# Softmax chain of a channel-attention kernel split by row block, with the square root on GpSimd, the row sums applied after the product with W, and the transposes of v as tasks of their own

## The chip, the cores and the metric

The kernel runs on one core of a Trainium2 chip. The time is the device time of one execution in microseconds (us). Of the core's engines these do the work here: TensorE (PE: matrix products and transposes, which it writes to PSUM), VectorE (DVE) and ScalarE (ACT) for elementwise work, GpSimd (POOL), which issues the loads, and SyncE (SP), which issues the stores. Each engine runs its own instructions strictly in the order in which the program lists them; a wait on one instruction holds all those behind it.

## The reference

Four batches of q, k and v, each 6336 x 256 in float32. Attention is over the 256 channels, not over the rows; a highway layer with two 256 x 256 matrices follows.

```python
qn = q / (np.linalg.norm(q, axis=1, keepdims=True) + 1e-06)
kn = k / (np.linalg.norm(k, axis=1, keepdims=True) + 1e-06)
s = kn.transpose(0, 2, 1) @ qn / tau
s = s - s.max(-1, keepdims=True)
a = np.exp(s)
a /= a.sum(-1, keepdims=True) + 1e-09
x = (v @ a).reshape(-1, 256)            # 25344 rows
H = np.maximum(x @ w_h, 0.0)
T = 1.0 / (1.0 + np.exp(-(x @ w_t + b_t)))
return T * H + (1.0 - T) * x
```

## The kernel before

**Stage 1** (`stage1`, lines 365 to 380) walks over the 6336 rows of a batch in 50 blocks of 128 (the last two of 96) and accumulates in two PSUM banks, `sg0` and `sg1`, one for each half of the 256 channels of k: the product of k and q (line 376, 256 columns), and the squares of k and of q (lines 377 and 378, 128 columns each), whose diagonals are the squared norms. q, k and v come in by loads of 8 row blocks (1 MB of float32 in memory, cast to float16 on the way), all issued by POOL in a fixed order, 8 of them in flight at most.

**The chain** (`plan_chain`, lines 386 to 639) then turns the sums of one batch into the operands `mr` of stage 2, once per batch. In order: four diagonals (DVE, line 413); the copy of the k-q product out of PSUM, which frees `sg0` and `sg1` for the next batch (ACT, line 433); the square root, for the first batch by one ACT instruction and a load of the table for the exponential (lines 440 and 441), for the other three by a shift, a first guess and three Newton steps on DVE, 13 small instructions in a row (lines 450 to 503); the reciprocal (518); two diagonal matrices (523), which a product with ones (`cqb`, PE, 535) spreads over the partitions; the scaling of the product (540, DVE) and the exponential of both halves (548, ACT), which also gives the row sums; their reciprocals (561, 571) and the normalised a (580 or 578), the first third of `mr`; four transposes of it (593), a copy out of PSUM (603 or 605), the product with both W (`ah`, 612), and its copy into the other two thirds of `mr` (623 or 625). Three of PSUM's users share the one bank `vt`: `cqb`, the four transposes, and the transposes of v of stage 2.

**Stage 2** (`plan_stage2`, lines 834 to 906) takes 25 groups of two row blocks per batch, 100 in all. Per group: transposes of v (line 657, two float16 channels at a time as one float32 word) into `vt`, their copy to `vtsb` (663 ACT or 665 DVE), and on PE three products of four matmuls each (line 686): h = x w_h, t = x w_t + b, and d, which completes x on top of relu(h)/2. ACT does relu (733) and tanh (747), DVE the two last steps (754 and 773); t begins as a copy of the bias (663 or 665) or, for some of the late groups, by a matmul (724). The transposes for the group two further on stand between the matmuls of h (`main_h`, line 692; `between` in `products`, line 680), so a task `h` also needs the bank `vt` free, and a buffer of `vtsb`.

**The order** of the instructions of each engine is found before the program is written, by `Plan.run` (lines 71 to 175): a simulation with a duration for every task, in which a free engine takes the ready task with the lowest key. Stage 2 has its group number g as key, stage 1 of the next batch keys spread over the groups of the batch before (`slot_of`), the chain -50, so it goes first wherever it is ready. A task that is ready only late on the chip still stands at its planned place. The tasks of POOL and SP, loads and stores, are kept in their listed order (`in_order`, line 85).

## Time and profile before

| | |
|---|---|
| median of 3 runs (lowest to highest) | 294.47 us (294.36 to 294.88) |
| the profiled execution: its time / the span of its instructions | 294.81 us / 293.0 us |
| busy: PE, ACT, DVE, POOL | 264.5, 192.4, 172.0, 48.8 us |
| mean TensorE clock granted, as a share of full speed | 0.974 |
| loads and stores | 39.20 MB (as float16) and 25.95 MB |

The page of the profile has one execution. "Busy" counts the time in which an engine has an instruction in work; matmuls overlap in the pipeline, so their durations (270 ns for 256 columns) are longer than the distance from one start to the next. In a timeline a row gives start, duration, engine, line, operation, output and inputs, and in brackets the idle time ahead of it and what ended it. A view by windows gives busy time per engine in a stretch of the span, the granted clock and the share of the DMA engines in use.

### The profile page before, as it was taken

To read this page: it belongs to the slowest core of one execution; us is meant where nothing else is said; L and a number is where in the kernel's file an instruction comes from. 1 tells how busy PE (TensorE), PEld (TensorE's weight loads), DVE (VectorE), ACT (ScalarE), POOL (GpSimd) and SP (SyncE) were. 2 spreads that over 40 slices of the span, in tenths; PEclk is the share of its full clock that TensorE was granted. 3 is DMA by queue.
4 is the path that set the end of the run, shared out by engine and by line. 5 is a ranking of instruction groups with operands and counts; after the bars stand their busy time and mean duration, and the time that the engine had idled before them with its cause. 6 is when DMAs were issued, how large, how long until landed. Compare 5 with 4: busy or idle time off the path is not lost.

```text
span 293.0 us, 6605 instructions
## 1 busy us (share of the span) xinstructions
PE 264.5 (90%) x2660; PEld 234.3 (80%) x2660; DVE 172.0 (59%) x343; ACT 192.4 (66%) x396; POOL 48.8 (17%) x96
## 2 busy tenths in 40 slices
PE   0787869999999989999999899999985899999993
PEld 0676847999999879999898789999973688888882
DVE  1000042455555874555658756655668599999995
ACT  1000042778877576888886667888784788889882
POOL 7212542221121221211211221111000010000000
PEclk9997988999999999999999999999997799999999
DMA  6999999999999999999999999999997264335444
GB/s 120 213 214 209 213 209 213 214 213 284 282 246 251 282 215 283 239 269 274 247 256 283 245 251 266 240 286 274 233 285 205 84 144 178 139 145 214 164 182 189
DMA packets 16687, 65.58 MB, mean 224 GB/s; under 512 B 1936, under 2 KB 3600, under 8 KB 13712
## 3 DMA queue, kind: packets, MB, share of 16 engines
q0 software_dynamic: 12608, 39.20, 67.9%
q1 hardware_dynamic: 4048, 25.95, 22.0%
q8 instruction: 21, 0.34, 0.5%
q14 instruction: 10, 0.08, 0.1%
HBM read 78.38 MB, written 25.95 MB: 356 GB/s over the span
## 4 chain that ended last, share of the span: by engine, by line
PE 75%; DMA 13%; DVE 8%; issue 1%; POOL 1%; ACT 1%; DVEq 0%; ACTq 0%; POOLq 0%
PE h L686 15%; PE t L686 14%; PE d L686 14%; PE sg L376 10%; PE vtps L657 8%; PE sg L377 5%; PE sg L378 5%; DMA k<-in_k_dram 5%; DMA q<-in_q_dram 5%; DMA btb<-in_moe_b_t_dram 3%; DVE pp L754 2%; DVE o L773 2%; PE t L724 1%; PE ah L612 1%; DVE gs L540 1%
## 5 line engine op out<-in xcount | busy, mean ns | idle before, releaser
L686 PEld LDWEIGHTS <-vtsb 128*128 128x128 f16 (+1 forms) x1200 | 114.8, 100 | 13.6 <-issue 2.2
L376 PE MATMUL sg<-q,k 128*128 128x256 f16 x384 | 96.1, 281 | 12.8 <-DMA k<-in_k_dram 12.8
L754 DVE SCALAR_TENSOR_TENSOR pp<-uu,d 128x512 f32<-128x512 f32 (+1 forms) x100 | 68.5, 685 | 52.2 <-PE d L686 50.2
L377 PE MATMUL sg<-k 128*128 128x128 f16 x384 | 86.4, 225 | 0.0
L378 PE MATMUL sg<-q 128*128 128x128 f16 x384 | 85.3, 222 | 0.0
L686 PE MATMUL h<-mr,vtsb 128*128 128x256 f16 (+1 forms) x400 | 82.8, 275 | 0.2
L747 ACT ACTIVATE uu<-t 128x512 f32<-128x512 f32 (+1 forms) x100 | 59.7, 597 | 27.3 <-PE t L686 26.8
L773 DVE SCALAR_TENSOR_TENSOR o<-h,pp 128x512 f32<-128x512 f32 x96 | 66.2, 691 | 3.1
L686 PE MATMUL d<-mr,vtsb 128*128 128x256 f16 (+1 forms) x400 | 60.5, 274 | 1.0 <-ACT d L733 1.0
L686 PE MATMUL t<-mr,vtsb 128*128 128x256 f16 (+1 forms) x400 | 60.8, 275 | 0.2
L733 ACT ACTIVATE d<-h 128x512 f32<-128x512 f32 (+1 forms) x100 | 59.5, 595 | 1.4 <-PE h L686 1.2
L657 PE MATMUL vtps<-ident,v 128*128 128x128 f32 x192 | 48.0, 278 | 3.6 <-DVE gs L540 3.4
L376 PEld LDWEIGHTS <-k 128*128 128x128 f16 x384 | 38.3, 100 | 15.2 <-DMA k<-in_k_dram 13.3
L378 PEld LDWEIGHTS <-q 128*128 128x128 f16 x384 | 38.6, 101 | 5.5
L377 PEld LDWEIGHTS <-k 128*128 128x128 f16 x384 | 38.6, 101 | 2.1 <-issue 0.3
L663 ACT COPY vtsb<-vtps 128x256 f32<-128x256 f32 (+1 forms) x91 | 33.4, 368 | 8.6 <-PE vtps L657 6.7
L663 ACT COPY t<-bias_all 128x512 f32<-128x512 f32 (+1 forms) x64 | 37.8, 590 | 2.0
L657 PEld LDWEIGHTS vtps<-ident,v 128*128 128x128 f32 x192 | 27.2, 142 | 8.9 <-DVE gs L540 4.3
L413 DVE SCALAR_TENSOR_TENSOR junk<-sg,ident 128x128 f32<-128x128 f32 x16 | 4.6, 290 | 35.6 <-PE sg L378 34.9
L274 POOL DMA_DIRECT2D v<-in_v_dram x24 | 12.8, 532 | 76.5 <-PE h L686 45.0
L440 ACT ACTIVATE inv<-x 128x4 f32<-128x4 f32 x1 | 0.2, 206 | 38.0 <-DVE junk L413 38.0
L274 POOL DMA_DIRECT2D k<-in_k_dram x25 | 13.3, 533 | 44.1 <-DMA k<-in_k_dram 16.0
(66 smaller groups left out, 121.5 us busy)
## 6 DMA issues: line engine op xcount, KB each, us to landing
out_dram<-o SPq DMA_DIRECT2D x23, 1024.0 KB, 8.9
v<-in_v_dram POOLq DMA_DIRECT2D x24, 512.0 KB, 20.7
q<-in_q_dram POOLq DMA_DIRECT2D x23, 512.0 KB, 21.7
k<-in_k_dram POOLq DMA_DIRECT2D x23, 512.0 KB, 20.6
out_dram<-o SPq DMA_DIRECT2D x2, 512.0 KB, 3.5
out_dram<-ot SPq DMA_DIRECT2D x4, 192.0 KB, 6.4
q<-in_q_dram POOLq DMA_DIRECT2D x2, 256.0 KB, 14.4
k<-in_k_dram POOLq DMA_DIRECT2D x2, 256.0 KB, 11.5
```

Of the source, the lines that this page charges most:

```text
L274: nc.gpsimd.dma_start(out=t[:, s : s + n, :], in_=main_rows(src)[:, j * CH + s : j * CH + s + n, :])
L376: nc.tensor.matmul(sg[c][:, 0:C], kc, qa, start=first, stop=False)
L377: nc.tensor.matmul(sg[c][:, C : C + P], kc, kc, start=False, stop=False)
L378: nc.tensor.matmul(sg[c][:, C + P : C + 2 * P], qa[:, cs], qa[:, cs], start=False, stop=last)
L413: nc.vector.scalar_tensor_tensor(out=st["junk"], in0=sg_t[b][c][:, off : off + P], scalar=0.0, in1=ident0, op0=AluOp.bypass, op1=AluOp.mul ...
L657: nc.tensor.transpose(ps[:, u, 0:nr], words, ident0[0:nr, 0:nr])
L663: nc.scalar.copy(out=out, in_=in_)
L686: nc.tensor.matmul(out[0:nr, u, :], vt[u][kt][:, 0:nr], mr[kt][:, col * C : (col + 1) * C], **flags(u, kt))
L733: nc.scalar.activation(out=d[0:nr, :, :], in_=ps_t["h", b, i][0:nr, :, :], func=Act.Relu, scale=0.5)
L747: nc.scalar.activation(out=uu[0:nr, :, :], in_=ps_t.pop(("t", b, i))[0:nr, :, :], func=Act.Tanh, scale=-0.5)
L754: nc.vector.scalar_tensor_tensor(out=pp[0:nr, :, :], in0=el.pop(("uu", b, i))[0:nr, :, :], scalar=1.0, in1=ps_t.pop(("d", b, i))[0:nr, :, ...
L773: nc.vector.scalar_tensor_tensor(out=ot, in0=ps_t.pop(("h", b, i))[0:nr, :, :], scalar=0.0, in1=el.pop(("pp", b, i))[0:nr, :, :], op0=AluO ...
```

## The change

Seven edits. (1) For every batch the square root is `x ** 0.5` on POOL, in two instructions of 128 x 2: one for the norms of q (`norm(0)`), one for those of k (`norm(2)`); the Newton steps, the square root on ACT and the table loaded for it go. (2) The diagonals are two tasks, q then k; the copies `gs` wait for the second. The reciprocals are two as well: that for q stands with the diagonal matrices ahead of `cqb`, that for k is only needed by the exponential. (3) Scaling, exponential, row sums and what follows are tasks by halves c = 0 and 1. (4) The exponentials themselves, in float32 and not yet divided by the row sums, are transposed (4 float32 transposes), copied to `et` and multiplied by W; the division is done by the copy of `ah` into `mr` (multiplied by `ri`), and the first third of `mr` takes the factor -0.5. (5) The copies of `et` and `ah` go to ACT or DVE, whichever the plan finds free. (6) The transposes of v are PE tasks of their own with key g - 1.6 (`LOOK`), `main_h` is its four matmuls alone, and no longer needs `vt`; the copy of `vt` has key g - 1.5, where it had g - 2.1. (7) In the plan POOL takes a ready task of the chain ahead of a load, and from the start of the fourth block before the last of a stage 1 until the second square root is done it issues no load (`holds`).

```diff
-LOOK = 2
+LOOK = 1.6
+POW = 1.0
...
         def pick(e):
-            if e in in_order:
-                lst = in_order[e]
-                return lst[-1] if lst and ready(lst[-1]) else None
-            return min(
+            best = min(
                 (x for x in avail[e] if ready(x)), key=lambda x: (x.key, x.n), default=None
             )
+            lst = in_order.get(e)
+            if best is None and lst and ready(lst[-1]) and not (e == "POOL" and held()):
+                return lst[-1]
+            return best
+
+        def held():
+            return any(
+                a.start is not None and (b.done is None or b.done > t + eps) for a, b in self.holds
             )
...
+        def norm(n):
+            nc.gpsimd.tensor_tensor(
+                out=st["inv"][:, n : n + 2], in0=st["x"][:, n : n + 2], in1=half, op=AluOp.pow
+            )
+
+        def recip(n):
+            inv = st["inv"][:, n : n + 2]
+            nc.vector.tensor_scalar(
+                out=inv, in0=inv, scalar1=1e-6, scalar2=None, op0=AluOp.add, op1=AluOp.bypass
+            )
+            nc.vector.reciprocal(out=inv, in_=inv)
...
-        x = dve(diagonals, 1.34, 1.4, [last, consts])
+        dq = dve(lambda: (diagonal(0), diagonal(1)), 0.75, 0.8, [last, consts])
+        nq = pool(lambda: norm(0), POW, POW + 0.2, [dq])
+        dk = dve(lambda: (diagonal(2), diagonal(3)), 0.75, 0.8, [dq])
+        nk = pool(lambda: norm(2), POW, POW + 0.2, [dk])
+        plan.holds.append((plan.tasks[plan.tasks.index(last) - 3], nk))
...
-        gs = act(copy_g, 0.58, 0.7, [diag], drop=[(first, "sg0"), (first, "sg1")])
...
-            last_steps = [floor, shift, guess] + [n1, n2, n3] * 3 + [root]
...
-        inv = x = several(last_steps + [eps, recip, lambda: dcat(0), lambda: dcat(1)], x)
+        gs = act(copy_g, 0.58, 0.7, [dk], drop=[(first, "sg0"), (first, "sg1")])
+        iq = dve(lambda: (recip(0), dcat()), 0.82, 0.92, [nq, dk])
+        ik = dve(lambda: recip(2), 0.3, 0.36, [nk])
...
-        cqb = x = pe(bcast, 0.85, [x], take=["vt"])
+        cqb = pe(bcast, 0.43, [iq], take=["vt"])
+        cqb.lat = 0.85
...
+        def soft(c):
...
+            nc.vector.tensor_scalar(
+                out=mr_t[b][c][:, 0:C],
+                in0=st["e"][:, c, :],
+                scalar1=st["ri"][:, c : c + 1],
+                scalar2=-0.5,
+                op0=AluOp.mult,
+                op1=AluOp.mult,
+            )
+
+        def trans(c):
+            if c == 0:
+                st["eps"] = new("vt", [P, 2, 2, P], f32, f"eps{b}")
+                st["et"] = small.tile([P, 2, C], f16, tag="et", name=f"et{b}")
+            for jk in range(2):
+                nc.tensor.transpose(
+                    st["eps"][:, c, jk, :], st["e"][:, c, bass.ts(jk, P)], ident0
+                )
+
+        def evac_et(c, e):
+            copy(e, st["et"][:, :, bass.ts(c, P)], st["eps"][:, c, :, :])
...
+        def evac_ah(c, e):
+            o, a, r = mr_t[b][c][:, C : 3 * C], st["ah", c], st["ri"][:, c : c + 1]
             if e == "ACT":
                 nc.scalar.mul(out=o, in_=a, mul=r)
...
+        sc = [dve(lambda c=c: scale(c), 0.37, 0.44, [cqb, gs]) for c in range(2)]
+        sc[1].drop = [(cqb, "vt")]
+        ex = [act(lambda c=c: exp(c), 0.65, 0.75, [sc[c], ik]) for c in range(2)]
+        ready, et = [], []
+        for c in range(2):
+            tr = pe(lambda c=c: trans(c), 0.22, [ex[c]] + et, take=["vt"] if c == 0 else [])
...
+            et.append(
+                either(
+                    lambda e, c=c: evac_et(c, e), (0.29, 0.35), (0.42, 0.47), [tr] + et,
...
+        for c in range(2):
+            ri = dve(lambda c=c: recip_sum(c), 0.3, 0.35, [ex[c]])
+            so = dve(
+                lambda c=c: soft(c), 0.3, 0.37, [ri] + ready[:1], take=["mr0", "mr1"] if c == 0 else []
+            )
...
+            fo = pe(lambda c=c: fold(c), 0.43, [et[c]] + w_ld, take=["h"])
+            ready.append(
+                either(
+                    lambda e, c=c: evac_ah(c, e), (0.5, 0.6), (0.63, 0.72), [fo, so],
...
-            if g < LOOK:
-                tr_own[g] = plan.add(
-                    "PE", g - 1.6, 0.22, 0.44, v_deps(g), lambda i=i: [f() for f in transposes(b, i)],
-                    take=["vt", "vtsb"], drop=drops("v", b, 2 * i + 1),
-                )
+            tr = plan.add(
+                "PE", g - LOOK, 0.22, 0.44, v_deps(g), lambda i=i: transposes(b, i),
+                take=["vt", "vtsb"], drop=drops("v", b, 2 * i + 1),
+            )
             ev = plan.add(
-                EV, g - LOOK - 0.1, (0.29, 0.35), (0.42, 0.47), [tr_own[g]],
-                lambda e, i=i: evac_vt(b, i, e), drop=[(tr_own[g], "vt")],
-            )
...
+                EV, g - LOOK + 0.1, (0.29, 0.35), (0.42, 0.47), [tr],
+                lambda e, i=i: evac_vt(b, i, e), drop=[(tr, "vt")],
+            )
...
-            h = tr_own[n] = plan.add(
-                "PE", g, 0.59 if ahead else 0.43, 0.8 if ahead else 0.64,
-                [ev] + ready[b] + (v_deps(n) if ahead else []) + ends_of[h_bank],
...
+            h = plan.add(
+                "PE", g, 0.435, 0.64, [ev] + ready[b] + ends_of[h_bank], lambda i=i: main_h(b, i),
+                take=[h_bank],
             )
...
-    nc.scalar.preload_act_table(Act.Sqrt)
+    nc.scalar.preload_act_table(Act.Exp)
```

More of the change, by code (lines that the diff above doesn't have):

```diff
@@ L384, with copy @@
     mr_own = {}
+    def copy(e, out, in_):
+        if e == "ACT":
+            nc.scalar.copy(out=out, in_=in_)
+        else:
+            nc.vector.tensor_copy(out=out, in_=in_)
     def plan_chain(b, first, last, key):
@@ L582, in soft @@
                 )
-        x = dve(lambda: (ri1(), ri2()), 0.34, 0.4, [es])
-        soft0 = dve(lambda: soft(0), 0.3, 0.35, [x], take=["mr0", "mr1"])
-        soft1 = (act if b else dve)(lambda: soft(1), 0.3, 0.4, [x, soft0])
-        mr_own[b] = soft0
-        def trans():
-            st["atps"] = atps = new("vt", [P, 2, 2, P], f16, f"atps{b}")
-            for ic in range(2):
-                for jk in range(2):
-                    nc.tensor.transpose(
-                        atps[:, jk, ic, :], mr_t[b][ic][:, bass.ts(jk, P)], ident
-                    )
@@ L597, in plan_chain @@
-        tr = pe(trans, 0.22, [soft0, soft1], take=["vt"])
-        def evac_at():
-            st["at"] = work.tile([P, 2, C], f16, tag="at", bufs=1, name=f"at{b}")
-            src = st["atps"].rearrange("p a b c -> p a (b c)")
-            if b:
-                nc.scalar.copy(out=st["at"], in_=src)
-            else:
-                nc.vector.tensor_copy(out=st["at"], in_=src)
-        x = (act if b else dve)(evac_at, 0.5, 0.6, [tr], drop=[(tr, "vt")])
-        def fold(ic):
-            st["ah", ic] = ah = new("h", [P, 2 * C], f32, f"ah{b}_{ic}")
-            for jk in range(2):
-                nc.tensor.matmul(
-                    ah,
-                    st["at"][:, jk, bass.ts(ic, P)],
-                    wht[:, jk, :],
-                    start=(jk == 0),
-                    stop=(jk == 1),
-                )
@@ L648, in transposes @@
     def transposes(b, i):
-        ps = new("vt", [P, 2, P], f32, f"vtps{b}_{i}")
+        vt_ps[(b, i)] = ps = new("vt", [P, 2, P], f32, f"vtps{b}_{i}")
         nr = rows(2 * i)
-        vt_ps[(b, i)] = ps
-        def one(u):
+        for u in range(2):
             words = sub("v", b, 2 * i + u).bitcast(f32)
             nc.tensor.transpose(ps[:, u, 0:nr], words, ident0[0:nr, 0:nr])
-        return [lambda: one(0), lambda: one(1)]
-    def copy(e, out, in_):
-        if e == "ACT":
-            nc.scalar.copy(out=out, in_=in_)
-        else:
-            nc.vector.tensor_copy(out=out, in_=in_)
     def evac_vt(b, i, e):
```

199 lines of the change are left out of this document (58 added, 141 removed).

## The prediction

> **What bounds the kernel now.** I read the page first, then the stages by windows, the waits of PE, and the timeline around the four chains. The windows name a dense stretch of both stages (60 to 80 us), a dense stretch of stage 2 alone (235 to 280), and two stretches at a low clock.
>
> ```profile
> span 293.0 us, 6605 instructions
> PE 264.5 (90%) x2660; PEld 234.3 (80%) x2660; DVE 172.0 (59%) x343; ACT 192.4 (66%) x396; POOL 48.8 (17%) x96
> ```
>
> ```profile
> 60.00:80.00 20.00, 20.00 (x219) 18.53 (x218) 11.03 (x16) 16.53 (x33) 3.16 (x6) 1.00 1.05 261
> 41.90:45.30 3.40, 3.30 (x22) 2.56 (x22) 2.40 (x7) 1.89 (x7) 2.14 (x4) 0.58 1.06 213
> 222.80:229.60 6.80, 5.92 (x29) 4.28 (x30) 5.03 (x12) 3.52 (x9) 0.00 (x0) 0.54 0.35 86
> 235.00:280.00 45.00, 45.00 (x401) 39.43 (x400) 41.79 (x66) 39.30 (x86) 0.44 (x1) 1.00 0.46 164
> ```
>
> After the length of a window come the busy times of PE, weight loads, DVE, ACT and POOL, the granted clock, the DMA share and GB/s. PE is busy for all 20.00 and all 45.00 us of the dense stretches at full clock: there PE is the bound, and only PE work or a PE stall changes the time. In the last one DVE (41.79) and ACT (39.30) have no more than 3 to 6 us of 45 to spare. In the two stretches at 0.58 and 0.54 the same matmuls go at half speed. What PE loses beside that, its waits tell:
>
> ```profile
> PE sg L376 <- DMA k<-in_k_dram: 12.8, 4, 8.9
> PE cqb L535 <- DVE dcat L523: 4.7, 2, 2.4
> PE vtps L657 <- DVE gs L540: 3.4, 3, 1.3
> PE d L686 <- ACT d L733: 1.0, 2, 0.7
> PE ah L612 <- ACT mr L623: 0.9, 1, 0.9
> ```
>
> The first row is the opening, in which the first batch's q and k arrive; the change leaves it alone. The other four, 10.0 us, all lie in the chains. So the chains cost idle PE time and, through the clock, half of what PE does in 3.3 + 5.9 us of busy time: 4.6 us. These 14.6 us are what the change can win.
>
> **Chain 0** (first batch) in the timeline:
>
> ```profile
> 38.61 0.22 PE L378 MATMUL sg<-q_t 96*128 96x128 f16 x1
> 39.72 0.29 DVE L413 SCALAR_TENSOR_TENSOR junk<-sg,ident 128x128 f32<-128x128 f32 x1
> 40.28 1.28 ACT L441 ACT_TABLE_LOAD   x1
> 41.25 0.70 PE L535 MATMUL cqb<-dcat,ones 128*128 128x256 f32 x2 [2.42 <-DVE dcat L523]
> 41.57 0.65 ACT L433 COPY gs<-sg 128x256 f32<-128x256 f32 x2
> 42.53 0.42 PE L376 MATMUL sg<-q,k 128*128 128x256 f16 x1
> ```
>
> PE stands for 2.42 us until `cqb`, and cannot begin the next batch's stage 1 (42.53) before the copies `gs` have freed `sg0` and `sg1` at 41.57 + 0.65. They stand behind the table load. In the change that load is gone and the copies follow the fourth diagonal (39.72, done near 40.05): they end near 40.7, and PE has work from about 40.75. `cqb` comes no sooner: diagonals of q until 39.4, the power (1.0 us, see below), reciprocal and `dcat`, so about 41.5. But it is covered by the first row blocks of the next batch; without that cover it would cost 0.3 us. PE stands 1.9 us instead of 2.42: **0.5 us** won. Whether the clock stays up is open: 2.42 and 2.3 us of idle time were followed by half speed, 1.3 us in chains 1 and 2 was not. 1.9 is nearer to the longer, so I count no gain; the other end is 1.65 more. By the Trainium skill, TensorE: Matmul & The Clock Gate, Why this matters for your kernels, only gaps of about 3 us or more bring the clock down; this trace disagrees (2.42 us was enough), and by that rule the sum would be 1.65 lower.
>
> **Chains 1 to 3** are alike; here is the last:
>
> ```profile
> 218.69 0.65 ACT L433 COPY gs<-sg 128x256 f32<-128x256 f32 x2
> 219.17 0.16 DVE L450 TENSOR_SCALAR x<-x 128x4 f32<-128x4 f32 x1
> 219.88 0.60 PE L686 MATMUL d<-mr,vtsb 128*128 128x256 f16 x4 [0.74 <-ACT d L733]
> 221.55 0.16 DVE L503 TENSOR_TENSOR inv<-x,y 128x4 f32<-128x4 f32 x1
> 222.56 0.68 DVE L773 SCALAR_TENSOR_TENSOR o<-h,pp 128x512 f32<-128x512 f32 x1
> 222.79 0.67 PE L535 MATMUL cqb<-dcat,ones 128*128 128x256 f32 x2 [2.32 <-DVE dcat L523]
> 223.75 0.74 DVE L540 TENSOR_TENSOR gs<-gs,cqb 128x256 f32<-128x256 f32 x2
> 224.55 0.48 PE L657 MATMUL vtps<-ident,v 128*128 128x128 f32 x1 [0.88 <-DVE gs L540]
> 231.98 0.59 PE L612 MATMUL ah<-wht,at 128*128 128x512 f16 x2 [0.89 <-ACT mr L623]
> ```
>
> The Newton block holds DVE from 219.17 to 221.7, with reciprocal and `dcat` to 222.6; the group's last step (line 773, 222.56) waits behind it, so no bank comes free, and PE stands 2.32 us. Then `cqb` keeps the bank `vt` until line 540 has read it, and the h behind it stands 0.88 us on its inserted transposes. The copies `gs` ahead of the relu cost 0.74, the second product with W 0.89. Idle in chain 3: 4.8 us, and 2.95 by the clock. Chains 1 and 2 show the `vt` wait alone, 1.2 to 1.3 each, and 0.3 on a relu, 2.8 in both: there PE has row blocks of the next batch to go on with.
>
> **What the change takes away there.** 2.55 us of Newton on DVE, per chain. The `vt` wait of h: h no longer needs `vt`, and the transposes are late only if `vt` is held longer than the 1.6 groups by which they run ahead, 2.6 us at the 1.6 us per group of the dense window (28 of line 754 in 45 us):
>
> ```profile
> L754 DVE SCALAR_TENSOR_TENSOR pp<-uu,d 128x512 f32<-128x512 f32 (+1 forms) x28 | 19.1, 683 | 2.2 <-PE d L686 1.3 <-ACT vtsb L663 0.4
> ```
>
>  In chains 1 and 2 I leave 0.3 each: **2.2 us** won, bounds 1.0 and 2.8. The chain's length itself is off the path, since groups of the batch before remain behind it; it is late for nobody.
>
> For chain 3, after which PE has only stage 2, I count engine time, since its work must come out of DVE and ACT:
>
> ```profile
> L413 DVE SCALAR_TENSOR_TENSOR junk<-sg,ident 128x128 f32<-128x128 f32 x16 | 4.6, 290 | 35.6 <-PE sg L378 34.9
> L548 ACT ACTIVATE e<-gs,inv 128x256 f32<-128x256 f32 x8 | 4.0, 501 | 11.2 <-DVE gs L540 11.2
> L548 ACT ACTIVATION_READ_ACCUMULATOR e<-gs,inv 128x1 f32 x8 | 1.5, 187 | 0.0
> L580 DVE TENSOR_SCALAR mr<-e,ri 128x256 f16<-128x256 f32 x5 | 1.7, 353 | 0.1
> ```
>
> Per chain, after: on DVE four diagonals 1.3 (0.33 apart in the timeline of chain 0), eight small steps at 0.2 (the distance of the Newton steps), `dcat` 0.5, scaling 0.74, two of line 580 0.7: 4.9 us. On ACT the copies 0.65 and two exponentials at 0.50 + 0.19: 2.0. The four copies that either may take cost 1.8 by the plan's durations. That is 8.7, or 4.35 per engine. PE does 1.7 of its own meanwhile (by starts: `cqb` 0.43, transposes 0.44, ah 0.87), and what DVE and ACT have spare, a tenth, gives 1.0 over some 10 us. There remain 1.7, and the 0.9 of the second ah, whose two banks `h` stay shared: 2.6 of idle time in pieces, none near 2.3, so no clock loss. From 4.8 + 2.95 that wins **5.2 us**; bounds 7.7 (all hidden) and 2.8 (idle time as now, at full clock).
>
> **What it adds.** First POOL's nearest rows and its loads in chain 0, then transposes in a row and between other matmuls:
>
> ```profile
> 2.72 0.29 POOL masks.py:199 TENSOR_SCALAR_AFFINE_SELECT ident<-ident 128x128 f32<-128x128 f32 x1
> 36.23 0.53 POOL L274 DMA_DIRECT2D q<-in_q_dram  x1 [1.32 <-DMA k<-in_k_dram]
> 40.53 0.53 POOL L274 DMA_DIRECT2D v<-in_v_dram  x1 [1.93 <-DMA k<-in_k_dram]
> ```
>
> ```profile
> 46.79 0.39 PE L657 MATMUL vtps<-ident,v 128*128 128x128 f32 x2
> 47.02 0.27 PE L376 MATMUL sg<-q,k 128*128 128x256 f16 x1
> 47.68 0.39 PE L593 MATMUL atps<-ident,mr 128*128 128x128 f16 x4
> 47.90 0.27 PE L376 MATMUL sg<-q,k 128*128 128x256 f16 x1
> 263.09 0.27 PE L657 MATMUL vtps<-ident,v 128*128 128x128 f32 x1
> 263.20 0.27 PE L686 MATMUL h<-mr,vtsb 128*128 128x256 f16 x1
> ```
>
> The power on POOL has no row. Its nearest is the 0.29 us of another elementwise instruction, a lower end; a load's issue takes 0.53; the upper end is the 2.3 us at which the gain is gone (below). I take 1.0. In chain 0 POOL issues no load from the last blocks of stage 1 until the second power, near 41.6, so two or three issues come up to 3.5 us later. Eight are in flight, and one lands about every 2.5 us (1.93 of waiting and 0.53 of issue), so the DMA queue does not run dry; without that cover a late row block costs PE the delay itself. SP's stores are untouched.
>
> The four float32 transposes cost 0.11 each (263.09 to 263.20) where the four float16 ones took 0.22 together (47.68 to 47.90): 0.22 more per chain, **0.9** in all. Two transposes of v in a row took 0.23 (46.79 to 47.02), against 2 x 0.11 between the matmuls: 0.01 in each of 98 groups, **1.0** (bounds 0 and 1.5). The narrower waits of `et` are covered by stage 2. The end, 288 to 293, stays.
>
> **The sum.** 293.0 - 0.5 - 2.2 - 5.2 + 0.9 + 1.0 = 287.0 us of span; 1.8 lie around it (294.81 - 293.0), and the profiled execution is 0.34 above the median: 288.8 - 0.3 = **288.5 us**. With every term at its worse bound it is 292.6 (0.5 + 1.0 + 2.8 won, 0.9 + 1.5 added), with every one at its better 282.7 (2.15 + 2.8 + 7.7 won, 0.9 added). They won't fall together; at half the distance either way this case runs from 285.6 to 290.5.
>
> **Rivals.** *All of chain 3 hidden and the clock kept in chain 0*: another 2.6 and 1.65 less, 284.3 us. For it speaks that only 1.7 + 0.9 remain by my count; against it that DVE has no more than 3.2 of 45 us free.
>
> *The loads become the bound of stage 1.* The DMA share stands at 1.05 from 60 to 80, and POOL's rows wait on landings. If row blocks are due 2.7 us sooner than now but arrive as before, what chains 0 to 2 win is lost: 291.2 us. Against it: after the opening, PE waits on no load at all, so there is some margin.
>
> *The power is slow, and takes Newton's place as what holds DVE.* The reciprocals wait for it in DVE's order, once for q and once for k, and lines 754 and 773 stand behind them. A power of P us beyond the planned 1.0 stops DVE 2 (P - 1) per chain: at P = 2.3 that is the 2.6 us that Newton took. From there nothing of chains 1 to 3 is won and the additions remain: 294.5 + 1.9 - 0.5 = 295.9, and each further us costs 2 in chain 3 and, half covered by row blocks, 1 in each of chains 1 and 2: 300 us at 3.3. For it: no row bounds the power from above. Against it: two elements per partition, where the row of 0.29 has 128. The Trainium skill, SBUF — State Buffer, Who interferes with whom, has a rule that works the same way: some DVE instructions (copies and tensor-scalar in a two-port mode among them) and a GpSimd instruction shut each other out for their whole length, so the k power would hold up the reciprocal of q; no run here shows it, and at 1.0 us it would put at most 1.0 more into a chain.
>
> *The loose transposes lose PE time in the dense stretches.* With one bank `vt` and a copy of it now ranked behind relu and tanh, a group may wait 0.1 us for it: 98 groups, 9.8 us, 298.3. Against it: the copies of `vt` take 0.4 us in groups of 1.6.
>
> **Chances.** Forecast 0.64, all hidden 0.08, loads 0.10, slow power 0.12, loose transposes 0.06. About 0.2% (0.6 us) is what a measurement of this kernel can tell from no change. Of the loads case a fifth falls within it; the first two and the rest of the third are faster: 0.80; within 0.2%: 0.02; the last two slower: 0.18. The range from 283.5 to 293.5 takes in the first three cases and leaves out the slower ones.
>
> **What would show it.** Chain 0: the first row block of the second batch starts near 40.8, ahead of `cqb` or close to it; the clock between 42 and 45 tells of the 1.65. Chains 1 to 3: no wait of PE on `cqb` above 1 us and none of a v transpose on line 540; the granted clock 1.00 through the last chain. POOL: two powers per chain near 1 us, the reciprocals directly behind, no load issue between. The dense window must still hold 1.6 us per group. I am wrong if the DVE rows behind the power show idle time above 2 us, if PE waits on loads after 40 us, or if a group in the dense stretch takes 1.7.

## The result, and the profile after

The changed kernel takes **283.48 us** (median of 4 runs, 283.25 to 284.01); the kernel before took 294.68 in the same comparison (294.36 to 295.24). The ratio is 0.962, with a 95% interval of 0.960 to 0.964. It is faster by 11.2 us where 6.0 were forecast, and ends 0.02 us below the low end of the range.

The profiled execution took 283.61 us, at a mean granted clock of 0.997 (0.974 before). From its page, the span, the busy times, the granted clock in 40 slices and the shares of the chain of work that ended last:

```profile
span 281.7 us, 6617 instructions
PE 258.4 (92%) x2660; PEld 231.8 (82%) x2660; DVE 184.5 (65%) x378; ACT 179.6 (64%) x341; POOL 54.7 (19%) x104
...
PEclk9999999999999999999999999999999999999998
...
DMA 47%; PE 43%; DVE 3%; POOL 3%; ACT 2%; issue 1%; DVEq 0%; POOLq 0%
```

No slice of the work is at a low clock any more (the last digit is the end of the span). All waits of PE in the changed kernel (total, times, longest):

```profile
PE sg L386 <- DMA k<-in_k_dram: 15.7, 8, 9.2
PE t L656 <- ACT gs L477: 1.1, 1, 1.1
PE vtps L605 <- ACT vtsb L398: 1.1, 2, 0.7
```

The waits on `cqb`, on the scaling of `gs` and on relu, 9.1 us before, are gone. Two of the waits that are left in the chains come from the copy `gs`, which frees the sums' banks: the 1.1, and 1.6 of the first row, in chain 0. Five windows of the changed kernel (PE, weight loads, DVE, ACT, POOL, clock, DMA share, GB/s), then two of them in the kernel before:

```profile
41.90:45.30 3.40, 3.40 (x39) 2.86 (x38) 2.31 (x9) 2.05 (x6) 2.69 (x6) 1.00 1.06 213
60.00:80.00 20.00, 20.00 (x220) 18.52 (x218) 14.86 (x25) 14.18 (x25) 3.03 (x6) 1.00 1.05 264
93.00:110.00 17.00, 16.89 (x174) 14.68 (x172) 13.46 (x40) 12.79 (x28) 4.61 (x8) 1.00 1.05 273
214.00:236.00 22.00, 19.68 (x172) 16.55 (x171) 18.21 (x47) 17.96 (x40) 2.48 (x4) 1.00 0.93 236
235.00:270.00 35.00, 35.00 (x313) 30.88 (x311) 31.08 (x54) 31.66 (x64) 0.00 (x0) 1.00 0.39 157
```

```profile
93.00:110.00 17.00, 15.46 (x170) 13.70 (x168) 13.13 (x43) 11.40 (x26) 3.60 (x7) 1.00 1.06 244
214.00:236.00 22.00, 17.05 (x123) 12.99 (x121) 15.83 (x49) 14.67 (x33) 1.57 (x3) 0.84 0.65 190
235.00:270.00 35.00, 35.00 (x312) 30.73 (x311) 32.51 (x51) 30.51 (x67) 0.44 (x1) 1.00 0.45 154
```

Around chain 3 (214 to 236) PE does 172 matmuls where it did 123; around chain 1 (93 to 110) it is busy but for 0.11 us. The dense stretches are what they were: 220 matmuls in 20 us (219 before) and 313 in 35 (312).

For a sum by stages, this table takes the distance from each matmul's start to the next, less what its form needs in the dense stretch (0.109 us for 256 columns of float16, half for 128, twice as much in float32), and adds up what is left. That is the time that PE loses to idle time and low clock. In the dense stretch from 60 to 80 us the same sum is 0.15. The chains are cut at 38.3 to 51, 93 to 110, 150 to 171 and 214 to 236 us; differences in the text are taken before rounding.

| lost by PE, us | chain 0 | 1 | 2 | 3 | elsewhere after 38.3 | span |
|---|---|---|---|---|---|---|
| before | 5.5 | 2.1 | 2.4 | 8.9 | 2.2 | 293.0 |
| after | 2.8 | 0.7 | 0.6 | 3.1 | 1.6 | 281.7 |
| Newton put back | 4.2 | 0.5 | 0.5 | 3.0 | 1.1 | 282.4 |
| v transposes put back | 3.7 | 0.8 | 0.8 | 2.7 | 1.8 | 282.6 |
| loose v transposes alone | 4.1 | 0.6 | 0.6 | 3.6 | 3.2 | 283.8 |
| power alone | 5.3 | 1.4 | 1.4 | 3.1 | 2.6 | 285.7 |
| both, chain not split | 5.1 | 0.9 | 0.9 | 3.5 | 1.8 | 284.4 |
| power three times | 3.7 | 1.9 | 1.9 | 4.5 | 1.2 | 286.2 |
| idle time of `cqb` filled | 2.9 | 2.1 | 2.5 | 7.1 | 2.2 | 290.8 |
| other bank for h, before | 5.3 | 2.1 | 2.4 | 4.9 | 2.0 | 289.2 |
| loose v transposes, banks later | 5.8 | 0.6 | 0.6 | 6.2 | 6.3 | 290.8 |

Of the 11.3 us of span, 2.7 came from chain 0, 3.3 from chains 1 and 2, 5.8 from chain 3 and 0.5 from elsewhere; the float32 transposes took back 0.9, and 0.1 more passes between the last matmul and the end. In the row of `cqb` filled, the useless matmuls, 2.2 us, count as work.

### The profile page after: what moved, and what is told of

Read it like the earlier page. It is cut to its first block, busy times and chain, and to the rows that moved or that the text cites. A ratio compares the mean times of both kernels' runs of the same rounds, so it can differ in the third digit from the quotient of the medians.

```text
span 281.7 us, 6617 instructions
## 1 busy us (share of the span) xinstructions
PE 258.4 (92%) x2660; PEld 231.8 (82%) x2660; DVE 184.5 (65%) x378; ACT 179.6 (64%) x341; POOL 54.7 (19%) x104
## 4 chain that ended last, share of the span: by engine, by line
DMA 47%; PE 43%; DVE 3%; POOL 3%; ACT 2%; issue 1%; DVEq 0%; POOLq 0%
DMA k<-in_k_dram 30%; DMA v<-in_v_dram 11%; PE h L625 9%; PE t L625 9%; PE d L625 8%; DMA q<-in_q_dram 6%; PE sg L386 5%; PE vtps L605 4%; PE sg L387 3%; PE sg L388 3%; PE t L656 1%; POOL inv L445 1%; DVE pp L686 1%; ACT d L665 1%; POOL k L284 1%
## 5 line engine op out<-in xcount | busy, mean ns | idle before, releaser
L625 PEld LDWEIGHTS <-vtsb 128*128 128x128 f16 (+1 forms) x1200 | 112.9, 99 | 14.3 <-issue 1.9
L386 PE MATMUL sg<-q,k 128*128 128x256 f16 x384 | 94.0, 276 | 15.8 <-DMA k<-in_k_dram 15.7
L387 PE MATMUL sg<-k 128*128 128x128 f16 x384 | 85.3, 222 | 0.0
L665 ACT ACTIVATE d<-h 128x512 f32<-128x512 f32 (+1 forms) x100 | 58.3, 583 | 22.1 <-PE h L625 21.8
L625 PE MATMUL h<-mr,vtsb 128*128 128x256 f16 (+1 forms) x400 | 59.8, 272 | 0.0
L400 DVE COPY vtsb<-vtps 128x256 f32<-128x256 f32 (+1 forms) x74 | 31.1, 421 | 26.9 <-PE vtps L605 26.6
L398 ACT COPY t<-bias_all 128x512 f32<-128x512 f32 (+1 forms) x78 | 46.2, 592 | 2.3
L605 PE MATMUL vtps<-ident,v 128*128 128x128 f32 x192 | 36.9, 274 | 1.3 <-ACT vtsb L398 1.1
L605 PEld LDWEIGHTS vtps<-ident,v 128*128 128x128 f32 x192 | 23.7, 141 | 3.7 <-ACT vtsb L398 1.6
L477 ACT COPY gs<-sg 128x256 f32<-128x256 f32 x8 | 2.6, 377 | 37.8 <-DVE junk L434 37.8
```

The costliest lines, as they stand in the source:

```text
L386: nc.tensor.matmul(sg[c][:, 0:C], kc, qa, start=first, stop=False)
L387: nc.tensor.matmul(sg[c][:, C : C + P], kc, kc, start=False, stop=False)
L398: nc.scalar.copy(out=out, in_=in_)
L400: nc.vector.tensor_copy(out=out, in_=in_)
L605: nc.tensor.transpose(ps[:, u, 0:nr], words, ident0[0:nr, 0:nr])
L625: nc.tensor.matmul(out[0:nr, u, :], vt[u][kt][:, 0:nr], mr[kt][:, col * C : (col + 1) * C], **flags(u, kt))
```

## The experiments

The theory was the forecast's: each part takes its own waits away, so that the parts' prices add up. The rival was that they take away the same wait, so that one of them nearly does.

### Undoing one part of the change

**Newton back on DVE**, for all four batches; the rest of the change stays:

```diff
-        nq = pool(lambda: norm(0), POW, POW + 0.2, [dq])
         dk = dve(lambda: (diagonal(2), diagonal(3)), 0.75, 0.8, [dq])
-        nk = pool(lambda: norm(2), POW, POW + 0.2, [dk])
-        plan.holds.append((plan.tasks[plan.tasks.index(last) - 3], nk))
+        nq = nk = dve(newton, 2.54, 2.6, [dk])
```

> The changed kernel with one part undone: the square root is again the 13 Newton instructions on DVE (for all four batches, all four norms at once, after the second pair of diagonals); everything else as changed. Theory (the Newton block on DVE is a main cause of the lost PE time): DVE is held about 2.6 us per chain again, the last steps of the groups wait behind it, and chain 3 loses some 2 to 5 us more (up to 3 of it by the clock), chains 1 and 2 at most 0.5 each, chain 0 nothing that the next batch's row blocks do not cover: 286 to 289 us. Rival (the split by halves and the loose transposes carry the gain, the power only comes along): within 0.6 us of the changed kernel, 283 to 284.

284.34 us (284.23 to 284.45), ratio 0.966 (0.963 to 0.969). That lies between the two expectations: with the rest in place the power on POOL is worth only 0.9 us. Chain 3 of this kernel, DVE's rows:

```profile
220.14 0.17 DVE L452 TENSOR_SCALAR x<-x 128x4 f32<-128x4 f32 x1
...
222.52 0.16 DVE L465 TENSOR_TENSOR inv<-x,y 128x4 f32<-128x4 f32 x1
222.60 0.68 DVE L721 SCALAR_TENSOR_TENSOR o<-h,pp 128x512 f32<-128x512 f32 x1
```

DVE is held for the same 2.5 us as before, and the group's last step (here line 721) stands behind it as it did. PE lost 3.0 us in this chain, no more than with the power (3.1); what Newton costs shows in chain 0. The block on DVE was there before; that it stopped PE was not its doing alone.

**The v transposes back between the matmuls of h**, with `vt` needed by h again; the rest of the change stays:

```diff
-LOOK = 1.6
+LOOK = 2
...
-            h = plan.add(
-                "PE", g, 0.435, 0.64, [ev] + ready[b] + ends_of[h_bank], lambda i=i: main_h(b, i),
-                take=[h_bank],
+            h = tr_own[n] = plan.add(
+                "PE", g, 0.59 if ahead else 0.43, 0.8 if ahead else 0.64,
+                [ev] + ready[b] + (v_deps(n) if ahead else []) + ends_of[h_bank],
+                lambda i=i, ahead=ahead: main_h(b, i, ahead),
+                take=[h_bank] + (["vt", "vtsb"] if ahead else []),
```

> The changed kernel with one part undone: the transposes of v stand again between the matmuls of h, so that h needs the bank vt (look-ahead 2, keys as before). Theory (the vt wait costs PE about 1 us in each of chains 1 to 3): 285.5 to 287.5 us, with PE waiting for a v transpose on the scaling by cqb again. Rival (the loose transposes are free of gain, or cost up to 1 us in the dense stretches): 282.5 to 283.7.

284.76 us (284.38 to 284.78), ratio 0.967 (0.964 to 0.971), again between the two expectations: loose transposes are worth 1.3 here. Its dense stretches, to be read against those above:

```profile
60.00:80.00 20.00, 20.00 (x221) 18.53 (x220) 11.24 (x17) 16.27 (x32) 3.31 (x7) 1.00 1.05 265
235.00:270.00 35.00, 35.00 (x312) 30.65 (x311) 32.31 (x50) 31.10 (x69) 0.00 (x0) 1.00 0.39 157
```

221 and 312 matmuls with the transposes between, 220 and 313 with them loose: the price of 0.01 us per group that the prediction put on loose transposes is not there.

### Making one part alone

**The loose v transposes alone**, on the kernel before:

```diff
-LOOK = 2
+LOOK = 1.6
...
+            tr = plan.add(
+                "PE", g - LOOK, 0.22, 0.44, v_deps(g), lambda i=i: transposes(b, i),
+                take=["vt", "vtsb"], drop=drops("v", b, 2 * i + 1),
+            )
...
+            h = plan.add(
+                "PE", g, 0.435, 0.64, [ev] + ready[b] + ends_of[h_bank], lambda i=i: main_h(b, i),
+                take=[h_bank],
```

> The kernel before with one part of the change alone: the transposes of v as PE tasks of their own (key g - 1.6, their copy g - 1.5), the chain as before. Theory (h waiting for the bank vt behind cqb costs 3.4 us in chains 1 to 3, and the Newton block the rest): 290 to 292 us, with the wait of PE on cqb in chain 3 and half clock after it still there. Rival A (with the Newton block in place the stall only moves): 294 to 295. Rival B (two float32 transposes in a row cost 0.01 to 0.1 us per group more): 295.5 or above, and the dense stretch of stage 2 above 1.61 us per group.

285.78 us (285.19 to 286.21), ratio 0.971 (0.967 to 0.975): 8.9 us won by this part alone, with Newton and the unsplit chain in place. It is 4 us below the lowest of the three expectations, none of which foresaw that this part nearly suffices.

**The power alone**, on the kernel before: one instruction of 128 x 4 on POOL in place of Newton and of the table load, with the hold on the loads:

```diff
+        def norm():
+            nc.gpsimd.tensor_tensor(out=st["inv"], in0=st["x"], in1=half, op=AluOp.pow)
+
+        step[0] += 1
+        x = plan.add("POOL", key + 1e-3 * step[0], 1.0, 1.2, [diag], norm)
+        plan.holds.append((plan.tasks[plan.tasks.index(last) - 3], x))
+        last_steps = []
```

> The kernel before with one part of the change alone: the square root as one power instruction of 128 x 4 on POOL, ahead of the loads, with the table of the exponential loaded at the start; chain, transposes and order else as before. Theory (Newton on DVE and the clock after it cost chain 3 some 5 us, the vt wait stays): 288 to 291 us. Rival (the vt wait and the copies are what counts, and taking 2.6 us off DVE only moves the stall there): 292.5 to 294.5. The power of 128 x 4 should take 0.7 to 1.0 us by the 0.71 of 128 x 2.

287.06 us (286.79 to 287.49), ratio 0.976 (0.972 to 0.979): 7.7 us, 0.9 below the range of the theory. The one instruction of 128 x 4 took 1.03 us.

**Both, with the chain not split** (the two edits above together):

> The kernel before with two parts of the change together: one power of 128 x 4 on POOL, and the transposes of v as tasks of their own; the chain stays unsplit (one task for all diagonals, both halves together, division before the transposes). Theory (power and loose transposes stand in for each other, since either keeps PE from standing behind DVE; what is left over is for the split): 284.5 to 286 us, hardly better than the loose transposes alone (285.8), and the changed kernel's last 1 to 2 us are the split's, most of it in chain 0. Rival (the two add up): 283.5 or below, and the split is worth nothing.

285.48 us (285.31 to 286.13), ratio 0.970 (0.967 to 0.973): 8.8 us. Alone the two win 8.9 and 7.7; together they win no more than the first. The split by halves with the division moved behind W (edits 2 to 5), which is what still stands between this kernel and the changed one, is worth the last 2.0 (the two were measured in different comparisons; the table's row is of an execution with a low stretch in chain 0, 0.6 us slower than the median). So the parts do not add up: they replace each other, and the rival holds.

### Why one part is nearly enough

Chain 3 with the loose transposes alone, rows of PE, then of DVE:

```profile
220.84 0.38 PE L712 MATMUL t<-btb,row 128*128 128x512 f16 x1 [0.62 <-ACT gs L433]
221.05 0.60 PE L681 MATMUL t<-mr,vtsb 128*128 128x256 f16 x4
221.49 0.60 PE L681 MATMUL h<-mr,vtsb 128*128 128x256 f16 x4
221.93 0.60 PE L681 MATMUL d<-mr,vtsb 128*128 128x256 f16 x4
...
223.97 0.70 PE L535 MATMUL cqb<-dcat,ones 128*128 128x256 f32 x2 [0.35 <-ACT vtsb L659]
```

```profile
220.31 0.16 DVE L450 TENSOR_SCALAR x<-x 128x4 f32<-128x4 f32 x1
...
222.69 0.16 DVE L503 TENSOR_TENSOR inv<-x,y 128x4 f32<-128x4 f32 x1
```

While Newton holds DVE, PE goes on with t, h and d. Two things differ from the kernel before. The first is where the chain falls: when the last matmul of the last stage 1 starts (216.52 us before, 217.07 after, 218.11 here), 252 matmuls of h were done before, and 268 in both others: four groups more, 6.4 us at 1.6 each. Stage 1 itself ends no sooner, since its loads come as they did; what chains 0 to 2 win shows as more of stage 2 behind it. The second follows from that: chain 3 begins with group 63 before, with group 67 now, and from `TAIL` = 65 on, h and t may also use the two banks that the sums have left (`h_tag`, line 702, and `t_tag`). Two runs tried that.

**Another bank for h in the kernel before**: the two banks are open from group 64 on, and the h of group 64 is the first to use one.

```diff
-TAIL = 65
+TAIL = 63
...
-        return "sg0" if g > TAIL and g % 3 == 2 else "h"
+        return "sg0" if g > TAIL and g % 3 == 1 else "h"
```

> The kernel before with one number and one remainder changed, nothing of the change: TAIL 63 instead of 65, and the h that take the bank sg0 are those with g % 3 == 1 instead of 2. The last chain falls on groups 63 to 65 there; with this the h of group 64 and the t of group 65 take the two banks that stage 1 of the last batch has left, where they stood behind DVE for a bank of the rings h and t. Newton, the transposes between the matmuls of h and the unsplit chain stay. Theory (in chain 3 PE stands on cqb because the two banks h are full while Newton holds DVE, and the kernels with loose transposes win there partly because their last chain falls on groups 66 and later, which have two banks more): the 2.3 us wait on cqb shrinks below 1 us, the clock stays full there: 289.5 to 292 us. Rival (the bank vt that h needs, or DVE itself, is the bound in chain 3, and more banks change nothing): 293.5 to 295.5.

291.19 us (290.98 to 291.64), ratio 0.989 (0.987 to 0.992). In its chain 3:

```profile
214.00:236.00 22.00, 18.93 (x156) 14.53 (x155) 17.95 (x52) 17.88 (x40) 1.57 (x3) 1.00 0.83 214
...
222.44 0.67 PE L535 MATMUL cqb<-dcat,ones 128*128 128x256 f32 x2 [0.55 <-DVE dcat L523]
```

The wait on `cqb` is 0.55 where it was 2.32, the clock 1.00 where it was 0.84, and the chain lost 4.9 us where it had lost 8.9. Nothing of the change is in it: the two banks two groups earlier give over half of the 5.8 us that the change wins in chain 3. The plan orders the instructions anew in every kernel, though, so some of this can be the order.

**Loose transposes, the banks later**: the run with loose transposes alone, with the banks open from group 72 on.

```diff
-TAIL = 65
+TAIL = 71
```

> The counterpart: the kernel before with loose transposes alone (285.8 us), and TAIL 71 instead of 65, so that the groups 66 to 71 in the last chain have only the banks of the rings h and t. Theory (the two banks carry part of what the loose transposes win in chain 3): PE stands 2 us or more on cqb or on an h in chain 3 again, and the late groups write the bias by copies longer: 288 to 291 us. Rival (loose transposes alone free PE in chain 3): 285.3 to 286.5 us.

292.59 us (292.36 to 293.82), ratio 0.995 (0.993 to 0.997): of 8.9 us, 2.0 are left. This row stands against the one with the banks from 66 on (second line):

```profile
235.00:270.00 35.00, 30.88 (x260) 25.60 (x259) 26.30 (x44) 27.13 (x55) 0.00 (x0) 1.00 0.32 128
...
235.00:270.00 35.00, 34.64 (x304) 29.86 (x303) 31.22 (x53) 29.37 (x61) 0.00 (x0) 1.00 0.39 157
```

It is more than expected, and not all of it is chain 3: by the table it loses 2.6 us more in chain 3, 3.0 more outside the chains, and 1.8 more in chain 0, which the edit doesn't touch and which had a low clock in this execution. `TAIL` also says from which group on a matmul may start t, so the order of the late groups differs. The 3.0 are in the late groups: behind 236 us PE stands 1.4 us on a relu and three times, 1.8 in all, on a bank for h. What set these off was not taken apart, so of the 6.8 us this run shows at most 2.6 to be the banks in chain 3.

### The price of a slow power

Each power three times, two of them into a spare tile, so that q's norms take 2.0 us and k's as long again:

```diff
+            for m in range(2):
+                nc.gpsimd.tensor_tensor(
+                    out=st["spare"][:, 2 * n + 2 * m : 2 * n + 2 * m + 2],
+                    in0=st["x"][:, n : n + 2], in1=half, op=AluOp.pow,
+                )
```

> The changed kernel with the suspected cost tripled: each power on POOL is done three times (twice into a spare tile, then into its place), so 2.1 us instead of 0.71; the plan still counts 1.0. The reciprocals wait in DVE's order, about 1.4 us more for q and 1.2 for k, 2.6 per chain: as long as Newton took in the kernel before. Slow-power rival of the prediction (what holds DVE as long as Newton did takes all of the gain in chains 1 to 3 away): 290 us or more, with PE waits of 2 us and more on cqb or on the last steps. Theory after the first four runs (with loose transposes PE has other work while DVE is held, so a held DVE costs little): 284.5 to 286.5 us.

289.51 us (288.01 to 290.78), ratio 0.983 (0.979 to 0.987), 0.5 below what the rival asked for and 3 above the theory. Its waits of PE, and DVE in chain 3:

```profile
PE h L632 <- DVE o L712: 2.0, 3, 0.8
PE cqb L492 <- DVE dcat L466: 1.9, 4, 1.0
```

```profile
223.19 0.17 DVE L458 TENSOR_SCALAR inv<-inv 128x2 f32<-128x2 f32 x1 [0.74 <-POOL inv L452]
...
225.15 0.17 DVE L458 TENSOR_SCALAR inv<-inv 128x2 f32<-128x2 f32 x1 [1.07 <-POOL inv L452]
```

DVE stands before both reciprocals and the rows behind them are late: the mechanism of the prediction's slow power, step by step. Its price: the four chains lose 12.1 us against 7.2 in the changed kernel, 4.9 for 1.3 us more per power, and the median is 6.0 higher. (The table has the fastest execution, at a mean clock of 1.000; the other three were at 0.986 to 0.990.) The rival priced 1.3 us more per power (2.3 for 1.0) at 7.4 us, 295.9 for 288.5; so its mechanism was right and its price somewhat high. It had no gain left at 2.3 us because the forecast's gain was smaller; at 2.0, 4.8 of the 11.2 are left.

### What the low clock costs

Ten matmuls of 128 x 256 that are overwritten stand ahead of `cqb` in chains 0 and 3 of the kernel before, so that PE idles less there:

```diff
+            for _ in range(10 if b in (0, B - 1) else 0):
+                nc.tensor.matmul(st["cqb"], ident, idle, start=True, stop=True)
```

> The kernel before with ten matmuls of a constant 128 x 256 float16 tile put ahead of the product cqb, into the same bank, in chains 0 and 3 alone: about 1.1 us of PE work without use, where PE stands idle for 2.4 and 2.3 us. All else as before, the waits too. Theory (the half clock after these two waits comes from the idle time of PE, and is a large part of what every variant wins): full clock in both chains, 4.6 us less: 289.5 to 291 us. Rival (the clock falls for another reason, or what is won by it is lost again because DVE and ACT are the bound there): 293.5 to 295.5.

291.95 us (291.09 to 293.12), ratio 0.993 (0.990 to 0.995): useless work made it faster by 2.4 us, between the two expectations. In the profiled execution chain 0 kept its clock and chain 3 did not, though its longest wait there was 1.1 us:

```profile
41.90:45.30 3.40, 3.29 (x40) 2.92 (x41) 2.40 (x7) 1.71 (x6) 2.12 (x4) 1.00 1.06 212
222.00:236.00 14.00, 12.05 (x88) 9.49 (x88) 10.18 (x21) 10.54 (x23) 1.04 (x2) 0.88 0.60 156
```

Executions of it whose mean clock is 0.999 or 1.000 have spans of 290.0 to 290.2 us. The kernel before had spans of 291.4 and 291.5 at a clock of 0.985 and of 292.9 to 293.2 at 0.973 to 0.975. By these spans the low clock costs it about 3 us, and some 8 of the 11.2 are idle time. It is an estimate: one execution with the matmuls, at 0.996, had a span of 289.3, so the clock is not all that differs.

### Two versions beyond the change

**The banks two groups later** in the changed kernel: the t of group 67, which stands 1.1 us on the copy `gs`, stays in its own bank.

```diff
-TAIL = 65
+TAIL = 67
```

> The changed kernel with TAIL 67 instead of 65: group 67 still takes its bank for t from the ring t, not the bank that stage 1 of the last batch has just left. In the changed kernel PE stands 1.1 us in chain 3 on a bias matmul into this bank, until the copies gs are out of it. Theory (that wait goes, and nothing takes its place): 282.3 to 283.0 us. Rival (the wait moves to the copies by the two engines that then write the bias): 283.2 to 284.

282.75 us (282.60 to 282.83), ratio 0.960 (0.958 to 0.963). The highest of its runs lies below the lowest of the changed kernel (283.25), and it is the best version here. The two were not run side by side, though: by the ratios it wins 0.5 us over the changed kernel, and their intervals overlap.

**The copies `gs` ahead of the diagonals**, on that version, so that the sums' banks come free sooner, and with a planned power of 0.75 us:

```diff
-        gs = act(copy_g, 0.58, 0.7, [dk], drop=[(first, "sg0"), (first, "sg1")])
+        gs = act(copy_g, 0.58, 0.7, [last])
+        plan.add("NONE", 0, 0, 0.01, [gs, dk], None, drop=[(first, "sg0"), (first, "sg1")])
```

> The changed kernel with TAIL 67 (282.75 us by itself) and two more edits: the copies gs start as soon as stage 1 ends, not after the diagonals of k (the banks sg are given back when both are done), and the plan counts the power with 0.75 us, near the 0.71 measured, instead of 1.0. Theory (in chain 0 PE waits for the copies until 40.4, in TAIL 67 for 1.7 us): the first row block of the second batch starts up to 0.4 us sooner, bounded by the load of k that lands near 40.4: 282.2 to 282.8 us. Rival (the load is the bound there, and an early copy delays relu or tanh in the other chains): 282.7 to 283.4.

283.75 us (283.48 to 283.82), ratio 0.964 (0.962 to 0.966): 1.0 slower than the version that it edits, which neither theory had. New in it is a wait of PE for copies of the bias by ACT, spread over chains 1 to 3; the version without the edit shows none of it:

```profile
PE t L626 <- ACT t L398: 2.4, 4, 0.6
```

That is near to the rival (ACT's other work is late), but the planned power was changed with it, so which of the two edits did it is open. Chain 0, in rows of ACT, DVE, POOL and PE:

```profile
38.83 0.65 ACT L477 COPY gs<-sg 128x256 f32<-128x256 f32 x2 [36.81 <-PE sg L388]
...
39.23 0.29 DVE L434 SCALAR_TENSOR_TENSOR junk<-sg,ident 128x128 f32<-128x128 f32 x1 [36.92 <-ACT gs L477]
...
40.03 1.48 POOL L445 TENSOR_TENSOR inv<-x,half 128x2 f32<-128x2 f32 x2 [3.31 <-DVE junk L434]
...
40.70 0.28 PE L386 MATMUL sg<-q,k 128*128 128x256 f16 x1 [1.69 <-DMA k<-in_k_dram]
```

The copies run sooner, and the diagonals now stand behind them: the first starts at 39.23, where it started at 38.61 without the edit, and the first row block at 40.70 instead of 40.45. But stage 1 itself ended 0.2 us later in this execution (its last matmul started at 38.80, not at 38.58), so PE's wait is as long as before, 1.69 against 1.65. The copies waited for the diagonals before, and the diagonals for the copies now; in chain 0 their order won nothing.

## Why the prediction was right, and where it was too small

**What held.** The direction and the mechanism: PE is the bound of the dense stretches, nearly all of the gain came from the chains, and the signs that were to bear the forecast out are in the trace. Of the three that were to refute it one came in part, a wait for loads after 40 us (see the rivals). Chain 0 in the changed kernel:

```profile
39.44 1.48 POOL L445 TENSOR_TENSOR inv<-x,half 128x2 f32<-128x2 f32 x2 [2.79 <-DVE junk L434]
39.78 0.70 ACT L477 COPY gs<-sg 128x256 f32<-128x256 f32 x2 [37.76 <-DVE junk L434]
40.20 0.17 DVE L451 TENSOR_SCALAR inv<-inv 128x2 f32<-128x2 f32 x1 [0.18 <-POOL inv L445]
40.45 0.28 PE L386 MATMUL sg<-q,k 128*128 128x256 f16 x1 [1.61 <-DMA k<-in_k_dram]
41.35 0.65 PE L485 MATMUL cqb<-dcat,ones 128*128 128x256 f32 x2
```

The first row block starts at 40.45 (40.75 forecast), `cqb` at 41.35 (41.5 forecast) and behind it. The wait of 1.61 is rather for the copies `gs` (0.70 from 39.78 on), which free the bank at about that time; in the version with `TAIL` = 67 the same wait of 1.7 bears their name.

**Term by term**, forecast against the table: chain 0 won 2.7, not 0.5. Chains 1 and 2 won 3.3, not 2.2. Chain 3 won 5.8, for 5.2: 3.1 us remain lost where the count of engine time gave 2.6. The float32 transposes cost 0.9 (each pair takes 0.38 to 0.40 us, the second starting 0.11 after the first). The loose transposes cost nothing, not 1.0.

**The steps that failed.** Three terms were mis-sized, all to the same side.

- Chain 0, "1.9 is nearer to the longer, so I count no gain" of the clock. The clock stayed up (1.00 from 41.9 to 45.3, 0.58 before): 1.4 of the 2.2 us that were missed, by 0.42 of the 3.30 us that PE was busy there. The wait itself shrank by 0.8, not 0.5. The rest is in small pieces. With the 1.9 us that it forecast the guess might have held: in the kernel with both parts and the chain not split, a wait of 1.79 at this place was followed by half clock in the profiled execution (see the last section).
- Loose transposes, "0.01 in each of 98 groups, 1.0". That came from a difference of 0.01 between two rows rounded to 0.01. The dense windows hold as many matmuls either way.
- Chains 1 and 2, "2.8 in both". What was left, 0.7 and 0.6 by the table, is not less than the 0.3 each of the forecast. What had been lost was more: 4.5 by the table, where the waits show 2.8. From start to start the waits of 1.25, 1.26 and 0.30 cost 1.41, 1.43 and 0.46, since the view counts idle time only from the end of a matmul's 0.27 us, and chain 2 lost another 0.7 in pieces too small for the view.

The missed 2.2, 1.1, 0.6 and 1.0, and 0.5 elsewhere, are, to rounding, the 5.3 us of span between 287.0 and 281.7.

**What held for another reason than given.** The prediction tied chain 3 to "2.55 us of Newton on DVE". Put back, Newton costs 0.9 us in all. What stopped PE was DVE held *and* no free bank: with DVE held as before, the changed kernel loses no more in chain 3, and two banks opened earlier take half of the loss away by themselves. The power breaks the first link (alone, it also brings the chain two groups later); the loose transposes, by bringing the chain to later groups, the second, without which they lose 2.6 more there. That h bound to `vt` was a third link is argued from the waits; no run took it away alone. Either part was nearly enough.

**The rivals.** *All of chain 3 hidden, and the clock kept* gave 284.3, nearest to the result, but by the wrong half: the clock was kept, chain 3 was not all hidden. *Loads*: half of it came. PE now waits 2.2 us on rows named after loads from 40 us on (1.6 of them the copies), the chain that ended last is 47% loads (13% before), and stage 1 ends 0.5 us later than before. But little was lost by it, since PE takes groups of stage 2 instead (four more by then). *Slow power*: a power takes 0.71 us:

```profile
L445 POOL TENSOR_TENSOR inv<-x,half x8: 690/712/777, 39.4 to 219.0; 128x2 f32<-128x2 f32 x8
L451 DVE TENSOR_SCALAR inv<-inv x8: 163/164/169, 40.2 to 220.3; 128x2 f32<-128x2 f32 x8
```

By the Trainium skill, SBUF — State Buffer, Who interferes with whom, the k power could have held up q's reciprocal. The row above shows no such thing: line 451 takes 164 ns with a power beside it in half of its eight instances, 169 at the longest. *Loose transposes that lose time in the dense stretches*: 20.00 of 20.00 and 35.00 of 35.00 us busy, no loss.

## What to carry to other kernels

Several edits that shorten the same stall replace each other: price each one alone and then given the others, and ask whether a cheaper one (here two banks opened two groups earlier) breaks the same chain of conditions. Where a stage is held by its loads, time won early comes back not as an earlier end of that stage but as later work already done, which can move a late stall onto other buffers. A term of 0.01 us in a hundred places needs a count over a long window, not a difference of two rounded rows.

## What the runs showed of the hardware

**Idle time and the clock.** The same idle time can cost the clock or not. With the loose transposes alone PE stands before `cqb` in chain 0 for as long as in the kernel before, 2.5 us against 2.42:

```profile
PE cqb L535 <- DVE dcat L523: 2.5, 1, 2.5
```

The clock stays at 1.00 there; it was 0.58 before. In the trace of before the low stretches are 3.41 us long in chain 0 and 6.83, twice that, in chain 3. In all thirteen traces every change of the clock lies a whole number of steps of 3.41 us after the first: there is a grid, which the kernel doesn't set. The Trainium skill, TensorE: Matmul & The Clock Gate, What's actually happening, says the same, a window of 3413 ns that runs freely. Here are cells of the grid that hold a wait, from the kernel before (chains 0 and 3), both parts unsplit (chain 0), `cqb` filled (chain 3), loose transposes alone (chain 0, two cells) and the changed kernel (chain 0):

```profile
39.02:42.43 3.41, 1.08 (x4) 0.51 (x5) 2.11 (x12) 2.13 (x4) 1.60 (x4) 1.00 1.24 211
219.92:223.34 3.42, 1.10 (x7) 0.64 (x6) 3.01 (x16) 1.01 (x2) 0.00 (x0) 1.00 1.04 298
37.82:41.24 3.42, 1.63 (x23) 1.38 (x21) 1.20 (x9) 0.70 (x2) 1.08 (x2) 1.00 1.21 202
219.60:223.02 3.42, 1.30 (x8) 0.54 (x6) 3.23 (x12) 0.35 (x1) 0.00 (x0) 1.00 1.04 316
36.91:40.32 3.41, 1.68 (x24) 1.42 (x21) 1.43 (x10) 0.49 (x2) 0.53 (x1) 1.00 1.20 204
40.32:43.74 3.42, 2.51 (x23) 1.81 (x24) 2.08 (x6) 3.03 (x8) 2.65 (x5) 1.00 1.08 212
37.65:41.06 3.41, 1.80 (x25) 1.53 (x23) 1.99 (x13) 0.70 (x2) 1.62 (x3) 1.00 1.21 202
```

After the first four the clock is 0.50, after the last three it stays at 1.00. PE was busy for 1.08 to 1.63 of the 3.41 us in the four, and for 1.68 and more in the three: with the loose transposes the 2.5 us of idle time fall over two cells. It holds for every cell from 36 to 275 us of the thirteen traces: the six with a fall behind them were at most 48% busy, all others at least 49%. It is not the whole rule, since in the openings two cells of 45 and 47% kept the clock. The rule of the Trainium skill, TensorE: Matmul & The Clock Gate, Why this matters for your kernels, by the length of a gap, weighed in the prediction, misses these rows: 2.5 us kept the clock, 1.79 lost it, and in chain 3 with `cqb` filled two waits of 1.1 and 1.0 in one cell lost it. So shorter idle pieces don't make a kernel safe by themselves; the changed kernel, with 1.61 us in one cell of chain 0, kept its clock (mean 0.997) by a small margin. The price is about 1.4 us for a low stretch in chain 0.

**A small power on GpSimd** takes 0.71 us for 128 x 2 elements in float32, two in a row 1.48 us, and one of 128 x 4 took 1.03. In chain 0 q's power ran from 39.44 to about 40.16, and the first step of the reciprocal on DVE began at 40.20.
